# Output tiles of the last block in column parts, each part with its own PSUM tile

## The chip, the cores and the metric

The kernel runs on one core of a Trainium2 chip. The metric is the device time of one execution in microseconds (us), median of several. The profile's span is some 1.8 us shorter than the timed execution (924.2 us against 926.03 for the same one).

Engines: TensorE (PE), VectorE (DVE), ScalarE (ACT), GpSimd (POOL), SyncE (SP, which issues most transfers). A q behind a name (SPq, ACTq) is that engine's instruction queue. "L539" is line 539 of the kernel.

## The reference

A layer norm, an attention over the last 512 keys of a cache with 32 heads of 192, and a feed-forward branch that gates it:

```python
xn = _layernorm(x, axis=-1)                       # x: 1 x 2048 x 640
s = _A_ref(xn, A_k_cache, A_v_cache, A_wq, A_wo)  # attention, last step: o @ wo
g = _silu(_B_ref(xn, B_w_gate, B_w_up, B_w_down))
return x + s * g
```

Only the last step matters here: the output projection `o @ wo`, the product with `g`, and the sum with `x`.

## The kernel before

The 2048 rows are 16 row tiles of 128, in 4 blocks of 4. I call them by block and tile: "3,1" is tile 1 of block 3, the last block. The heads are handled in 16 pairs. Each pair's share of the projection is added to `sacc`; for the last pair it comes straight from PSUM. For blocks 2 and 3 the last two pairs are accumulated together in PSUM (`late`), so such a tile takes 12 matmuls of 320 columns. By then `sacc` holds `sum * g + x` of the earlier pairs, so a tile is finished by one product and one sum:

```python
def wo_last(b, qt, eng):
    i, t = last * NB + b, 4 * b + qt
    ...
    split = b == NB - 1 and qt == 3
    sc = None if split else mm_tile() if b >= 2 and qt % 2 == 0 else sc_tile()
    ps = [(mm_tile()[:, 0, :] if split else sc[:, n, :])[:, 0:HD] for n in range(2)]
    for n, cols in enumerate(halves):
        if late(i):
            wo_mm(ps[n], i - NB, qt, n, end=False)
        wo_mm(ps[n], i, qt, n, first=not late(i))
        if split:
            nc.vector.tensor_tensor(s_f[:, n, :], ps[n], g2[:, t, cols], ALU.mult)
            nc.vector.tensor_tensor(ob[:, cols], s_f[:, n, :], sacc[:, t, cols], ALU.add)
            (nc.scalar if n else nc.sync).dma_start(out=..., in_=ob[:, cols])
    if split:
        return
    nc.vector.tensor_tensor(s_f[:], sc[:, :, 0:HD], g2[:, t, :]..., ALU.mult)   # product
    eng.tensor_tensor(ob[:], s_f[:]..., sacc[:, t, :], ALU.add)                 # sum
    stores.append((t, ob))
...
for b in (2, 3):
    for qt in range(4):
        store(0 if (b, qt) == (3, 3) else 3)
        wo_last(b, qt, V if b == 3 and qt % 2 == 0 else G)      # V VectorE, G GpSimd
```

`sc_tile()` and `mm_tile()` hand out two kinds of PSUM tile, two of each, which together fill PSUM. Only the last tile, 3,3, works in two halves, both in `mm` tiles.

The softmax here doesn't subtract the row's maximum and nothing guards it: scores larger than these inputs give would overflow.

## Time and profile before

| What | Number |
|---|---|
| Time, median | 925.96 us (3 runs, 925.85 to 926.03) |
| Span of the profile | 924.2 us |
| TensorE busy | 916.6 us, 99% |
| GpSimd busy | 100.1 us, 11%, most of it at the end |
| First matmul of tile 3,0 | at 912.44 us |
| Last store issued | at 921.39 us |

The part that the change touches is what I call the **tail**: from the first matmul of tile 3,0 to the end of the span, 924.2 - 912.44 = 11.76 us. It is read from two places of one profile, and the span has one decimal, so it is good to about 0.05 us. The prediction below shows the lines of this stretch.

### The profile page before, as it was taken

The page shows a single profiled execution, that of the slowest core. Times are in us where ns is not written, and L with a number is a line of the kernel's source. Part 1 is how long each engine was busy: PE and PEld are TensorE (multiplying, and loading weights), DVE is VectorE, ACT ScalarE, POOL GpSimd, SP SyncE. Part 2 cuts the span into 40 slices and gives each one's busy share as a digit, 9 for nine tenths or more (in the row PEclk, how much of TensorE's full clock was granted, in tenths as well). Part 3 has the DMA queues.
Part 4 walks back from the last instruction along what each step waited for, and adds up shares of the span by engine and source line. Part 5 has one row for each costly group of instructions (what it writes and reads, how often), then busy time and mean ns, then how long its engine had stood idle before and what let it go on. Part 6 is the DMA issues. An engine that isn't in the chain of part 4 may idle for free.

```text
span 924.2 us, 25783 instructions
## 1 busy us (share of the span) xinstructions
PE 916.6 (99%) x11101; PEld 622.6 (67%) x11101; DVE 576.1 (62%) x844; ACT 473.8 (51%) x847; POOL 100.1 (11%) x387
## 2 busy tenths in 40 slices
PE   9999999999999999999999999999999999999997
PEld 5455555575858585868686767676767777776665
DVE  6433331467676767676666667676767676767655
ACT  4222223546464656555556465655555555656561
POOL 0000000000000000000000000000000000002977
PEclk9999999999999999999999999999999999999999
DMA  9321510044544443444636252635371717162624
GB/s 297 74 54 35 114 35 1 1 81 86 83 83 80 86 80 86 72 94 66 100 59 107 57 109 53 112 50 116 45 121 40 126 37 129 35 132 74 145 47 140
DMA packets 243810, 77.18 MB, mean 84 GB/s; under 512 B 224624, under 2 KB 243696, under 8 KB 243696
## 3 DMA queue, kind: packets, MB, share of 16 engines
q1 hardware_dynamic: 242640, 74.72, 40.7%
q8 instruction: 87, 1.43, 0.7%
q10 hardware_dynamic: 1056, 0.82, 0.3%
q14 instruction: 27, 0.22, 0.1%
HBM read 39.45 MB, written 2.62 MB: 46 GB/s over the span
## 4 chain that ended last, share of the span: by engine, by line
PE 98%; DMA 1%; DVE 1%; ACTq 0%; issue 0%; ACT 0%; DVEq 0%
PE mm L430 22%; PE sc L565 19%; PE sc L444 18%; PE mm L470 16%; PE sc L276 11%; PE mm L298 6%; PE sc L539 3%; PE mm L522 2%; PE mm L539 1%; DMA wu_sb<-in_B_w_up_dram 1%; PE mm L276 0%; PE mm L311 0%; PE sc L522 0%; PE sc L470 0%; PE mm L444 0%
## 5 line engine op out<-in xcount | busy, mean ns | idle before, releaser
L448 ACT ACTIVATE p_t<-sc 128x1024 bf16<-128x1024 f32 x254 | 253.0, 1022 | 128.9 <-PE sc L444 128.9
L435 DVE TENSOR_REDUCE qT<-mm 128x512 bf16<-128x1024 f32 x189 | 230.9, 1223 | 91.6 <-PE mm L430 89.2
L500 ACT ACTIVATE O_b<-mm,r 128x192 bf16<-128x192 f32 x486 | 164.6, 421 | 183.6 <-issue 162.4
L430 PE MATMUL mm<-xnT,wq_p 64*128 64x512 bf16 x1890 | 240.0, 376 | 0.0
L590 DVE TENSOR_TENSOR sacc<-sacc,sc 128x640 f32<-128x640 f32 x200 | 164.2, 821 | 89.5 <-PE sc L565 89.5
L565 PE MATMUL sc<-wo_p,OT_b 64*128 64x320 bf16 x2592 | 217.0, 296 | 0.0
L444 PE MATMUL sc<-qT,khat 64*128 64x512 bf16 x1524 | 198.1, 376 | 0.5 <-DVE sacc L588 0.5
L470 PE MATMUL mm<-V_p,p_t 64*128 64x193 bf16 x3520 | 186.2, 242 | 0.1
L470 PEld LDWEIGHTS <-p_t 64*128 64x128 bf16 x3584 | 162.4, 93 | 12.9 <-issue 0.6
L430 PEld LDWEIGHTS <-wq_p 64*128 64x128 bf16 x1890 | 104.7, 94 | 95.7 <-issue 0.5
L565 PEld LDWEIGHTS <-OT_b 64*128 64x128 bf16 x2592 | 139.4, 94 | 22.2
L444 PEld LDWEIGHTS <-khat 64*128 64x128 bf16 x1536 | 85.1, 94 | 80.1 <-issue 0.7
L553 POOL MEMSET turn_t<- 128x1 f32 x328 | 32.2, 98 | 697.0 <-PE mm L470 474.6
L284 DVE TENSOR_TENSOR hT<-sc,sg 128x512 bf16<-128x512 f32 x46 | 31.7, 690 | 85.2 <-ACT sg L283 85.1
L283 ACT ACTIVATE sg<-sc 128x512 bf16<-128x512 f32 x46 | 27.3, 596 | 72.4 <-PE sc L276 72.4
L276 PE MATMUL sc<-xnT,wu_sb 128*128 128x512 bf16 (+1 forms) x260 | 59.1, 354 | 0.2 <-DMA wu_sb<-in_B_w_up_dram 0.2
L276 PE MATMUL sc<-xnT,wg_sb 128*128 128x512 bf16 (+1 forms) x260 | 59.2, 354 | 0.1
L298 PE MATMUL mm<-wd_sb,hT 128*128 128x320 bf16 x384 | 56.6, 299 | 0.0
L489 DVE RECIPROCAL r<-mm 128x4 f32<-128x4 f32 x124 | 22.7, 183 | 47.8 <-PE mm L470 36.3
L298 PEld LDWEIGHTS <-hT 128*128 128x128 bf16 x384 | 37.6, 98 | 18.9
L276 PEld LDWEIGHTS <-wu_sb 128*128 128x128 bf16 x285 | 26.3, 98 | 27.2 <-DMA wu_sb<-in_B_w_up_dram 0.4
L276 PEld LDWEIGHTS <-wg_sb 128*128 128x128 bf16 x285 | 26.4, 98 | 23.1 <-issue 0.2
(68 smaller groups left out, 372.9 us busy)
## 6 DMA issues: line engine op xcount, KB each, us to landing
wo_p<-in_A_wo_dram SPq DMA_DIRECT2D x16, 480.0 KB, 4.2
K_p<-in_A_k_cache_dram SPq DMA_DIRECT2D x32, 192.0 KB, 3.3
V_p<-in_A_v_cache_dram SPq DMA_DIRECT2D x32, 192.0 KB, 3.1
wq_p<-in_A_wq_dram SPq DMA_DIRECT2D x64, 80.0 KB, 3.2
wq_p<-in_A_wq_dram SPq DMA_DIRECT2D x16, 160.0 KB, 3.4
x_r<-in_A_x_dram SPq DMA_DIRECT2D x16, 160.0 KB, 3.9
x_t<-in_A_x_dram SPq DMA_DIRECT2D x14, 160.0 KB, 3.0
OT_b<-O_b SPq DMA_TRANSPOSE x124, 2.8
```

Of the source, the lines that this page charges most:

```text
L276: nc.tensor.matmul(out, w_sb[:, c, f * P : (f + 1) * P], xnT[:, c, qc], start=(c == 0), stop=(c == NC - 1),)
L298: nc.tensor.matmul(dn[:, 0:HD], hTs[b][:, f, ti * P : (ti + 1) * P], wd_sb[:, f, cols], start=(f == 0), stop=(f == NF - 1),)
L430: nc.tensor.matmul(q_ps[:, h, :], pairs[pr]["wq"][r, c, j * P : (j + 1) * P], xnT[r, c, b * 512 : (b + 1) * 512], start=(c == 0), stop=(c ...
L435: nc.vector.reduce_sum(qTs[i][:, j, :], q_ps[:, :, :].rearrange("p h n -> p n h"), axis=AX.X)
L444: nc.tensor.matmul(sc[:, h, :], khat[r, j, ks], qT[r, j, :], start=(j == 0), stop=(j == 2))
L448: nc.scalar.activation(p_t[:, :, :], sc[:, :, :], ACT.Exp, scale=scale)
L470: m = nc.tensor.matmul(acc[:, k, h * 256 : h * 256 + Dh + 1], Ps[i][kc][r, h, qt * P : (qt + 1) * P], V_p[r, kc, h, 0 : Dh + 1], start=(p ...
L500: nc.scalar.activation(O_b[:, qt, h, :], a_k[:, h, 0:Dh], ACT.Copy, scale=r[:, k, h, :])
L539: nc.tensor.matmul(ps, OTs[i][:, 3 * qt + j, :], pairs[i // NB]["wo"][:, j, n * HD : (n + 1) * HD], start=(first and j == 0), stop=(end an ...
L553: st["turn"] = nc.gpsimd.memset(turn_t[:], 0.0)
L565: m = nc.tensor.matmul(ps[:, n, 0:HD], OTs[i][r, 3 * qt + j, :], pairs[i // NB]["wo"][r, j, n * HD : (n + 1) * HD], start=(turn == 0 and j ...
L590: nc.vector.tensor_tensor(s_t, s_t, sc[:, :, 0:HD], ALU.add)
```

## The change

Its intent: finish the last rows sooner after TensorE is done, by working on pieces. All four tiles of block 3 are made in column parts. Every part has its own PSUM tile, the first of a tile an `mm`, the second an `sc`. VectorE multiplies each part as soon as it is there, and the sums are dealt out by part to GpSimd (G) and VectorE (V). The last tile is cut into 384 and 256 columns, the 256 part's store on ScalarE's queue. The core of the diff:

```diff
+    def wo_parts(qt, parts):
+        i, t, c0 = NS - 1, 4 * (NB - 1) + qt, 0
+        ob = finp.tile([P, D], bf, name="ob", bufs=4)
+        s_f = finp.tile([P, D], f32, name="s_f", tag="s_f", bufs=4)
+        for n, (width, eng, queue) in enumerate(parts):
+            cols, c0 = slice(c0, c0 + width), c0 + width
+            ps = (sc_tile() if n else mm_tile())[:, 0, 0:width]
+            wo_cols(ps, i - NB, qt, cols, end=False)
+            wo_cols(ps, i, qt, cols, first=False)
+            nc.vector.tensor_tensor(s_f[:, cols], ps, g2[:, t, cols], ALU.mult)
+            eng.tensor_tensor(ob[:, cols], s_f[:, cols], sacc[:, t, cols], ALU.add)
+            if queue:
+                queue.dma_start(out=out2[t * P : (t + 1) * P, cols], in_=ob[:, cols])
+        if not queue:
+            stores.append((t, ob))
...
-    for b in (2, 3):
-        for qt in range(4):
-            store(0 if (b, qt) == (3, 3) else 3)
-            wo_last(b, qt, V if b == 3 and qt % 2 == 0 else G)
+    for qt in range(4):
+        store(3)
+        wo_last(2, qt)
+    for qt, engs in enumerate(((G, V), (G, G), (V, G))):
+        store(2 - qt)
+        wo_parts(qt, [(HD, eng, None) for eng in engs])
+    store(0)
+    wo_parts(3, ((384, G, nc.sync), (D - 384, V, nc.scalar)))
```

The rest of the diff only takes the split case out of `wo_last` and gives the matmul helper its columns. The stores of finished rows are also asked for earlier (`store(2 - qt)` where it was `store(3)`).

More of the change, by code (lines that the diff above doesn't have):

```diff
@@ L535, in late, with wo_cols @@
         return i // NB >= NPAIR - 2 and i % NB >= 2
-    def wo_mm(ps, i, qt, n, first=True, end=True):
+    def wo_cols(ps, i, qt, cols, first=True, end=True):
         for j in range(3):
             nc.tensor.matmul(
-                ps, OTs[i][:, 3 * qt + j, :], pairs[i // NB]["wo"][:, j, n * HD : (n + 1) * HD],
+                ps, OTs[i][:, 3 * qt + j, :], pairs[i // NB]["wo"][:, j, cols],
                 start=(first and j == 0), stop=(end and j == 2),
             )
+    HALVES = [slice(n * HD, (n + 1) * HD) for n in range(2)]
     def follows(m, earlier):
@@ L602, in wo_full @@
         for n in range(2):
-            wo_mm(sc[:, n, 0:HD], i, qt, n)
+            wo_cols(sc[:, n, 0:HD], i, qt, HALVES[n])
         s_t = sacc[:, t, :].rearrange("p (n d) -> p n d", n=2)
@@ L618, with wo_last @@
     stores = []
-    def wo_last(b, qt, eng):
+    def wo_last(b, qt):
         i, t = last * NB + b, 4 * b + qt
@@ L623, in wo_last @@
         s_f = finp.tile([P, 2, HD], f32, name="s_f", bufs=4)
-        halves = [slice(n * HD, (n + 1) * HD) for n in range(2)]
-        split = b == NB - 1 and qt == 3
-        sc = None if split else mm_tile() if b >= 2 and qt % 2 == 0 else sc_tile()
-        ps = [(mm_tile()[:, 0, :] if split else sc[:, n, :])[:, 0:HD] for n in range(2)]
-        for n, cols in enumerate(halves):
-            if late(i):
-                wo_mm(ps[n], i - NB, qt, n, end=False)
-            wo_mm(ps[n], i, qt, n, first=not late(i))
-            if split:
-                nc.vector.tensor_tensor(s_f[:, n, :], ps[n], g2[:, t, cols], ALU.mult)
-                nc.vector.tensor_tensor(ob[:, cols], s_f[:, n, :], sacc[:, t, cols], ALU.add)
-                (nc.scalar if n else nc.sync).dma_start(
-                    out=out2[t * P : (t + 1) * P, cols], in_=ob[:, cols]
-                )
-        if split:
-            return
+        sc = mm_tile() if b == 2 and qt % 2 == 0 else sc_tile()
+        for n, cols in enumerate(HALVES):
+            if late(i):
+                wo_cols(sc[:, n, 0:HD], i - NB, qt, cols, end=False)
+            wo_cols(sc[:, n, 0:HD], i, qt, cols, first=not late(i))
         nc.vector.tensor_tensor(
@@ L642, in wo_last @@
         )
-        eng.tensor_tensor(ob[:], s_f[:].rearrange("p n d -> p (n d)"), sacc[:, t, :], ALU.add)
+        G.tensor_tensor(ob[:], s_f[:].rearrange("p n d -> p (n d)"), sacc[:, t, :], ALU.add)
         stores.append((t, ob))
+    def wo_parts(qt, parts):
[13 more added lines that the diff above has]
+            stores.append((t, ob))
     def store(left):
@@ L720 @@
         for k in range(2):
-            wo_last(b, 2 * q2 + k, G)
+            wo_last(b, 2 * q2 + k)
         if more:
             pv_full(i + more[0], more[1])
-    for b in (2, 3):
-        for qt in range(4):
-            store(0 if (b, qt) == (3, 3) else 3)
-            wo_last(b, qt, V if b == 3 and qt % 2 == 0 else G)
+    for qt in range(4):
[6 more added lines that the diff above has]
+    wo_parts(3, ((384, G, nc.sync), (D - 384, V, nc.scalar)))
 _INS = ['A_x', 'A_k_cache', 'A_v_cache', 'A_wq', 'A_wo', 'B_x', 'B_w_gate', 'B_w_up', 'B_w_down']
```

## The prediction

> **What bounds the kernel now.** I read the page first (busy shares, slices), then the chain that ended last in the stretch from 905 us, then the timeline of that stretch, then the DMA issues. The page:
>
> ```profile
> span 924.2 us, 25783 instructions
> PE 916.6 (99%) x11101; PEld 622.6 (67%) x11101; DVE 576.1 (62%) x844; ACT 473.8 (51%) x847; POOL 100.1 (11%) x387
> POOL 0000000000000000000000000000000000002977
> ...
> PEclk9999999999999999999999999999999999999999
> ```
>
> TensorE is busy for 99% of the span at full clock, so all but about 8 us is TensorE work, and the change leaves that work alone: it still runs 48 projection matmuls for block 3 with the same weight loads and the same total of columns. GpSimd (POOL) is busy for 11% of the span, nearly all of it in the last four slices (23 us each): that is the stage the change touches. The end of the chain (columns: start us, length us, what):
>
> ```profile
> 912.60 1.63 PE mm L539 x12
> 914.23 1.63 PE sc L539 x12
> 915.86 1.64 PE mm L539 x12
> 917.50 0.03 issue
> ...
> 917.60 0.84 DVE s_f L640
> ...
> 918.46 0.04 DVE ob L643
> ...
> 919.43 0.49 DVE s_f L633
> 919.94 0.49 DVE ob L634
> 920.43 0.41 DVE s_f L633
> 920.87 0.49 DVE ob L634
> ```
>
> TensorE carries the chain until 917.50. From there VectorE carries it to 921.36, then the last store runs to 924.2. So only 6.7 us of 924.2 are open to this change, 0.7%. The timeline shows what VectorE and GpSimd do there (start us, us, engine, line, operation):
>
> ```profile
> 909.75 6.04 POOL L643 TENSOR_TENSOR ob<-s_f,sacc 128x640 bf16<-128x640 f32 x4
> 915.20 1.27 DVE L643 TENSOR_TENSOR ob<-s_f,sacc 128x640 bf16<-128x640 f32 x1
> 916.40 0.81 DVE L640 TENSOR_TENSOR s_f<-sc,g 128x640 f32<-128x640 f32 x1
> 917.29 1.54 POOL L643 TENSOR_TENSOR ob<-s_f,sacc 128x640 bf16<-128x640 f32 x1 [1.50 <-DVE s_f L640]
> 918.46 1.05 DVE L643 TENSOR_TENSOR ob<-s_f,sacc 128x640 bf16<-128x640 f32 x1
> 918.48 0.57 PE L539 MATMUL mm<-wo_p,OT_l 128*128 128x320 bf16 x3 [0.17 <-DVE s_f L640]
> 921.39 0.37 ACTq L635 DMA_DIRECT2D out_dram<-ob  x1
> ```
>
> Three things are to be seen. GpSimd is booked without a gap until 915.79 (909.75 + 6.04), with the sums of block 2. The two VectorE sums of 640 columns took 1.27 and 1.05 us, though two of 320 columns took 0.49 each. And TensorE lost a little before its last half tile: the first matmul there waited for VectorE to read tile 3,2.
>
> **What the skill says.** (1) The Trainium skill, "SBUF — State Buffer", section "SBUF: two separate sides": VectorE and GpSimd share a port pair under an exclusive lock; a VectorE instruction with two SBUF inputs and a GpSimd one that reads SBUF do not share, whichever starts first has it for its whole length. The trace agrees, closely: the first 640 sum ended at 916.47, 0.68 us after GpSimd's at 915.79; the second at 919.51, also 0.68 us after GpSimd's at 918.83. A VectorE sum that meets GpSimd therefore sits until GpSimd is done and then needs 0.68 us. The products `s_f`, one input from PSUM, took 0.82 us with GpSimd busy or not. (2) "GPSIMD Engine Reference", section "3.1 Elementwise — side-by-side cycle accounting": about 2.6 cycles per element for two inputs against about 1 on VectorE. The trace: 1.50 us from start to start on GpSimd against 0.82 us on VectorE for 640 columns. (3) "Perfetto Trace Analysis", section "DMA Instruction — HWDGE (DVE, Sync)": an issue's span leaves out the movement of data, and completion to HBM can be long. The trace: 0.37 us of issue, 1.6 us to landing.
>
> **The change, part by part.** Durations used: a half tile (six matmuls of 320) is 0.815 us on TensorE (1.63/2). I take 0.98 and 0.65 us for 384 and 256 columns, in proportion. A product starts 0.27 us after the next matmuls of TensorE could start (912.44 to 912.71). A 320 product lasts 0.48 us, the next independent instruction starts 0.41 us after it, a dependent sum 0.51 us after. A free VectorE sum of 320 is 0.49 us; after GpSimd lets go it needs half of 0.68, 0.34 us, and 0.27 us for 256 columns. For GpSimd no 320 sum is in the trace: from 1.50 us with a small fixed part I estimate 0.80 us for 320 and 0.95 for 384.
>
> Removed: the two 640 sums on VectorE in tiles 3,0 and 3,2 (1.27 + 1.05 us), and one 640 sum on GpSimd. Added: two 320 sums and one 256 sum on VectorE, four 320 sums and one 384 sum on GpSimd. VectorE's sums fall from 1920 columns to 896, GpSimd's rise from 640 to 1664, about 2.5 us more work for an engine that is not free before 915.79. Six instructions more in the pair of engines, and no more DMA.
>
> What moves on TensorE: with six parts ring-buffered over two kinds of PSUM tile, each part waits for a reader two tiles back. The wait of 0.17 us (0.33 with the refill, 918.48 against 918.15) goes away. TensorE's last group should end at 917.33 + 1.63 = 918.96 instead of 919.30. That alone would be 0.3 us.
>
> What happens after it, if the lock changes hands at each instruction (case A). Product 3,0 first part 913.53, second 914.34; its VectorE sum starts 914.85, is held to 915.79, ends 916.13. GpSimd's 3,0 sum then runs to 916.95. Products 3,1 at 916.15 and 916.58, 3,2 first at 917.0. VectorE's 3,2 sum starts 917.5, is held by GpSimd's 3,1 first part to 917.75, ends 918.09. GpSimd's second 3,1 part ends 918.89, 3,2 second 919.69. Product of 384 at 918.58, of 256 at 919.23 (TensorE end 918.96 + 0.27), ready 919.64. The last VectorE sum gets the lock at 919.69 and ends 919.96; GpSimd's 384 sum then ends 920.92. Or the other way about: GpSimd first, then 0.27 us for VectorE, 920.93. Either way the last issue starts near 920.97 instead of 921.39. From issue to end I keep 2.81 us (924.2 - 921.39). Sum: 923.78, or **-0.4 us**.
>
> **Rivals.** Case B, a wait takes the place of the one removed: GpSimd's next instruction starts before the lock is free, since its starts are 1.50 us apart and its spans 1.55 us. A waiting VectorE then loses to every queued GpSimd sum. VectorE's 3,0 sum would be held to 916.57 (915.77 + 0.80) and end 916.91; products 3,1 at 916.83 and 917.24, 3,2 first at 917.65; its sum is held by both GpSimd parts of 3,1 to 918.93 and ends 919.27; last products 919.6 and 920.1; GpSimd's 3,2 part to 920.52, 384 part to 921.43, VectorE's last sum 921.70, issue 921.74. That is **+0.35 us**. For it: the overlapping spans. Against it: in the trace, VectorE's held sums ended 0.68 us after the holder in both cases; but no second GpSimd instruction was queued then, so this does not decide.
>
> Case C, little contention: GpSimd runs back to back from 915.79 (917.37, 918.17, 918.97 at the ends of its parts but for the first), the 384 sum waits for its product at 919.13 and ends 920.08; VectorE's last sum ends 920.35, issue 920.39, **-1.0 us**. For it: this is what the split into narrower parts aims at. Against it: both VectorE sums of the old kernel that could meet GpSimd did.
>
> Case D: the landing of the smaller store hides or undoes it. The last store falls from 80 to 64 KB and the other grows to 96 KB; issue to landing was 1.6 us at 80 KB and 1.8 at 160 KB, so 16 KB is worth about 0.03 us. I leave it out.
>
> **Range and chances.** I give A 0.45, B 0.35, C 0.20: -0.18 + 0.12 - 0.20 = -0.26, so 925.96 - 0.26 = 925.7 us. The range runs from C (924.9) to B with the spread of the old runs, 0.1 us (926.4). A change of 2% is 18.5 us, more than the whole tail. Faster by over 2%: 0.005; within 2%: 0.99; slower by over 2%: 0.005.
>
> **What would show it.** Everything up to about 912.4 us must look as before. Right: no TensorE wait at the last half tile; VectorE's sums lengthened when GpSimd is busy, ending 0.34 us after it; the last issue near 921.0. If VectorE's 3,0 sum ends near 916.9, it is B; if all three VectorE sums are near 0.5 us, C. The prediction is wrong if a GpSimd sum of 320 costs much more than 0.8 us, if products with a PSUM input are held as well, or if the stretch from last issue to end is not 2.8 us.

## The result, and the profile after

The changed kernel took 925.26 us (median of 5 runs, 925.09 to 925.64), the kernel before 925.85 (5 runs, 925.52 to 926.03). The ratio is 0.9994, 95% interval 0.998 to 1.0007. A ratio is the mean time of one kernel's fast runs over that of the other's of the same rounds, so not quite the ratio of the medians quoted. By the 2% measure this is the same time; what is left is a difference of about 0.6 us, with both kernels scattered by 0.5 us.

The page after, its head and GpSimd's row of busy tenths:

```profile
span 923.8 us, 25792 instructions
...
POOL 0000000000000000000000000000000000002978
```

0.4 us less span, and one tenth more of GpSimd in the last slice. Before taking the 0.4 us for the change, look where it arises. TensorE's third set of transposes, ten microseconds into the kernel, and its first matmuls of tile 3,0, first in the profile before (start us, length us, engine, line, operation):

```profile
10.63 0.45 PE L264 MATMUL tp<-ident,xn 128*128 128x128 bf16 x5
...
912.44 0.57 PE L539 MATMUL mm<-wo_p,OT_l 128*128 128x320 bf16 x3
```

and in the profile after:

```profile
10.36 0.45 PE L264 MATMUL tp<-ident,xn 128*128 128x128 bf16 x5
...
912.16 0.57 PE L539 MATMUL mm<-wo_p,OT_l 128*128 128x320 bf16 x3
```

A lead of 0.27 us is there after 10 us, in code that the change does not touch, and 0.28 us at tile 3,0. TensorE, 99% busy in between, carries it to the end. Over all the profiles tile 3,0 starts anywhere from 911.99 to 912.97 us. That scatter is larger than the effect sought, so from here on the tail is compared: 923.8 - 912.16 = **11.64 us** after, 11.76 us before. In these two profiles the tail is 0.12 us shorter.

The end of the chain of work that ended last, after (start us, length us, what):

```profile
915.58 0.83 PE mm L539 x6
916.41 0.03 issue
...
917.94 0.42 DVE ob L649
918.36 0.48 DVE s_f L648
...
919.11 0.85 POOL ob L649
919.97 1.13 POOLq L766
```

Before, TensorE handed over to VectorE at 917.50, 5.06 us after the start of tile 3,0, and VectorE carried the chain to its last sum. Now TensorE leaves the chain at 916.41, 4.25 us after that start, and the end goes through GpSimd. The timeline of the two engines after:

```profile
913.97 1.57 POOL L634 TENSOR_TENSOR ob<-s_f,sacc 128x640 bf16<-128x640 f32 x1
914.51 2.20 DVE L649 TENSOR_TENSOR ob<-s_f,sacc 128x320 bf16<-128x320 f32 x1
915.47 0.90 POOL L649 TENSOR_TENSOR ob<-s_f,sacc 128x320 bf16<-128x320 f32 x1
...
917.19 3.91 POOL L649 TENSOR_TENSOR ob<-s_f,sacc 128x320 bf16<-128x320 f32 x4 [0.83 <-DVE s_f L648]
...
919.66 0.58 DVE L649 TENSOR_TENSOR ob<-s_f,sacc 128x256 bf16<-128x256 f32 x1
920.28 0.37 ACTq L651 DMA_DIRECT2D out_dram<-ob  x1
921.12 0.33 SPq L651 DMA_DIRECT2D out_dram<-ob  x1
```

VectorE's first sum, 320 columns, takes 2.20 us; one of the same size took 0.49 us before, where nothing was in its way. It ends at 916.71, 0.34 us after GpSimd's second instruction of this list, at 916.37. So it was held through two GpSimd instructions. Meanwhile VectorE makes no product for GpSimd, which then stands idle for 0.83 us. The last issue, on SyncE's queue, comes 8.96 us after the start of tile 3,0; before it was 921.39 - 912.44 = 8.95. So up to the last issue nothing is won here; that it is this hold which costs the gain, the profiles with a shorter hold below show. The 0.12 us lie after the last issue, in a stretch of 2.68 us (2.81 before) that scatters by about 0.1 us over the profiles below.

### The profile page after: what moved, and what is told of

Its sections match the earlier page's. It is cut to its first block, busy times and chain, and to the rows that moved or that the text cites. A ratio compares the mean times of both kernels' runs of the same rounds, so it can differ in the third digit from the quotient of the medians.

```text
span 923.8 us, 25792 instructions
## 1 busy us (share of the span) xinstructions
PE 916.7 (99%) x11101; PEld 626.0 (68%) x11101; DVE 576.2 (62%) x846; ACT 473.8 (51%) x847; POOL 103.3 (11%) x391
## 4 chain that ended last, share of the span: by engine, by line
PE 98%; DMA 1%; DVE 0%; POOLq 0%; issue 0%; POOL 0%; DVEq 0%
PE mm L430 22%; PE sc L567 19%; PE sc L444 18%; PE mm L470 16%; PE sc L276 11%; PE mm L298 6%; PE sc L539 3%; PE mm L522 2%; PE mm L539 1%; DMA wg_sb<-in_B_w_gate_dram 1%; PE mm L276 0%; PE mm L311 0%; DMA x_t<-in_A_x_dram 0%; PE sc L522 0%; PE sc L470 0%; DVE s_f L648 0%
```

## The experiments

They ran in three batches of four, each batch on one chip with the kernel before timed beside it. "Tail" is as defined above; "last issue" is the issue of the last store, counted from the start of tile 3,0.

| Run | What | Tail, us | Last issue, us | Median time, us | Ratio |
|---|---|---|---|---|---|
| (before) | first profile | 11.76 | 8.95 | 925.96 | |
| e6_b_again | before, again | 11.73 | 8.98 | 925.93 | 1.0001 |
| (after) | first profile | 11.64 | 8.96 | 925.26 | 0.9994 |
| e1_after_again | changed, again | 11.15 | 8.40 | 925.29 | 0.9993 |
| e12_after_third | changed | 11.11 | 8.42 | (one run) | |
| e13_after_fourth | changed | 11.10 | 8.37 | (one run) | |
| e2_psum_only | TensorE's wait removed alone | 11.77 | 8.96 | 926.19 | 1.0002 |
| e3_last_v | last sums both on VectorE | 11.07 | 8.38 | 925.77 | 0.9997 |
| e7_halves | last tile 320 + 320 | 11.08 | 8.34 | 925.53 | 0.9996 |
| e5_first_gg | first sum to GpSimd | 11.55 | 8.90 | 925.92 | 0.9999 |
| e8_product_in_psum | changed, VectorE sums from PSUM | 10.69 | 7.97 | 924.89 | 0.9988 |
| e10_gv | that, 3,2 exchanged | 10.75 | 7.79 | 925.37 | 0.9992 |
| e9_b_product_in_psum | before, VectorE sums from PSUM | 11.84 | 9.05 | 925.92 | 1.0001 |
| e11_b_psum_own | that, without TensorE's wait | 11.57 | 8.86 | 925.85 | 0.9997 |

The 95% intervals are about 0.0013 to either side, so one ratio alone rarely decides, and I go by the tails. Each tail is read from one profile; two profiles of the same code in which the engines took the same turns differ by 0.01 to 0.05 us. By "lock theory" the expectations mean what the prediction says under (1): a VectorE sum with two inputs in SBUF and a GpSimd sum wait for each other.

### Both kernels again: e1_after_again, e6_b_again

No edit in either.

> The changed kernel once more, unaltered. I measure the tail: from the first projection matmul of tile 3,0 to the end of the span; it was 11.76 us before (924.2 - 912.44) and 11.64 us changed (923.8 - 912.16). Theory 1: the tail is the same from run to run, and of the 0.4 us between the two profiles only 0.12 us belongs to the change; the other 0.28 us was there at tile 3,0 already and comes from the first loads of the kernel. Then the tail here is 11.64 within 0.05 us, while the start of tile 3,0 may lie anywhere from 912.1 to 912.5, and the ratio of times is near 0.9998. Rival: the change saves about 0.5 us in a usual run, as the medians 925.85 and 925.26 say; then the ratio is 0.9994 to 0.9995 again and the tail shorter than 11.5 us.

> The kernel before once more, as a control with its own profile. Theory 1: tail 11.76 us within 0.05, start of tile 3,0 from 912.1 to 912.5 us, ratio 1.000 within 0.0003. Rival (its first profile was not typical): a tail longer than 11.9 us.

The control came out as expected in tail and ratio: 11.73 us and 1.0001. The start of tile 3,0 did not: it was 912.97 us here and 912.75 in e1_after_again, both outside the 912.1 to 912.5 that I had written. For the changed kernel theory 1, that the tail is the same from run to run, fell: it was 11.15 us, 0.49 us shorter than in the first profile of the same code, and the ratio 0.9993. The lines of VectorE's first and last sums, and of the last issue, in this run:

```profile
915.11 1.34 DVE L649 TENSOR_TENSOR ob<-s_f,sacc 128x320 bf16<-128x320 f32 x1
...
919.93 1.18 DVE L649 TENSOR_TENSOR ob<-s_f,sacc 128x256 bf16<-128x256 f32 x1
...
921.15 0.37 ACTq L651 DMA_DIRECT2D out_dram<-ob  x1
```

The same instruction, started at the same place (2.36 us after tile 3,0 against 2.35), took 1.34 us instead of 2.20. GpSimd's line shows why:

```profile
914.57 1.53 POOL L634 TENSOR_TENSOR ob<-s_f,sacc 128x640 bf16<-128x640 f32 x1
916.06 1.11 POOL L649 TENSOR_TENSOR ob<-s_f,sacc 128x320 bf16<-128x320 f32 x1
```

VectorE's sum ended at 916.45, 0.35 us after GpSimd's 640 sum at 916.10: it got its turn at the first change of instruction. Now GpSimd's next sum was the one held, 1.11 us instead of some 0.86. The last sum, 256 columns, ends 0.28 us after GpSimd's 384 sum (919.85 + 0.98 = 920.83), held as well. So the tail of the changed kernel has two lengths, depending on who gets the turn. The rival of theory 1, that the change usually saves more than its first profile shows, stands.

### How often: e12_after_third, e13_after_fourth

The changed kernel twice more, one look each.

> The changed kernel again, for one more look at how VectorE's sum of tile 3,0 and GpSimd take turns. In the first profile it was passed over at the change from GpSimd's last 640 sum to its first 320 sum and took 2.20 us (tail 11.64); in three others with the same code up to there it got its turn and took 1.34 to 1.35 us (tail 11.07 to 11.15). If the turn is left to chance, either of the two may show; if only two lengths are possible, nothing between 1.4 and 2.1 us does, and the tail goes with it.

> As the run before it: VectorE's sum of tile 3,0 takes either 1.35 us, with a tail near 11.15, or 2.20 us, with a tail near 11.64; the longer one should come with longer GpSimd spans (1.57 us for 640 columns) and the shorter with 1.53 to 1.54[...].

The first VectorE sum in e12_after_third, then in e13_after_fourth:

```profile
914.35 1.37 DVE L649 TENSOR_TENSOR ob<-s_f,sacc 128x320 bf16<-128x320 f32 x1
```

```profile
914.76 1.32 DVE L649 TENSOR_TENSOR ob<-s_f,sacc 128x320 bf16<-128x320 f32 x1
```

The sum took 1.37 and 1.32 us, the tails were 11.11 and 11.10 us. So of four looks at the changed kernel one has the long hold, three the short one; in e3_last_v and e7_halves, whose code is the same up to there, it took 1.35 us as well. GpSimd's 640-column spans were 1.57 us in the one long case and 1.52 to 1.56 in the short ones. The order is as I expected, but the 1.56 of e12_after_third misses the 1.53 to 1.54 that I had written for the short hold, and 1.56 against 1.57 with one long case is too little to show that GpSimd's length decides. What decides the turn stays open.

### TensorE's wait alone: e2_psum_only

On the kernel before:

```diff
-ps = [(mm_tile()[:, 0, :] if split else sc[:, n, :])[:, 0:HD] for n in range(2)]
+ps = [((sc_tile() if n else mm_tile())[:, 0, :] if split else sc[:, n, :])[:, 0:HD] for n in range(2)]
```

> The kernel before, with only the second half of the last tile put into the other kind of PSUM tile, so that TensorE no longer waits for the reader of tile 3,2; sums and stores are as before. Theory 1: the wait goes and TensorE ends 0.33 us sooner, but VectorE is behind by then (its last four instructions ran without a gap from 919.43 us), so the tail stays at 11.76 us within 0.05. Rival: the removed wait is what the change gains; then the tail is 11.43 us.

```profile
918.14 0.57 PE L539 MATMUL sc<-wo_p,OT_l 128*128 128x320 bf16 x3
```

The wait went: the last half tile's matmuls start at 918.14, 5.71 us after tile 3,0, instead of 6.04. VectorE's last four instructions did not move (919.42 - 912.43 = 6.99 us against 919.43 - 912.44 = 6.99), and the tail is 11.77 us. Taking this wait away gains nothing by itself, because VectorE was behind. (Only this half tile was moved; the own PSUM tiles of the other parts are not tested here.)

### The last sum and the widths: e3_last_v, e7_halves

```diff
-wo_parts(3, ((384, G, nc.sync), (D - 384, V, nc.scalar)))
+wo_parts(3, ((384, V, nc.sync), (D - 384, V, nc.scalar)))     # e3_last_v
+wo_parts(3, ((HD, G, nc.sync), (HD, V, nc.scalar)))           # e7_halves
```

> The changed kernel, with the 384-column sum of the last tile moved from GpSimd to VectorE. In the changed kernel that sum ended last, 8.92 us after the start of tile 3,0. Lock theory: VectorE's 384 sum becomes ready about 7.15 us after the start of tile 3,0 while GpSimd works on tile 3,2 until 7.8, so it is held, ends near 8.2, and the 256 product and sum follow to about 9.0: the tail stays between 11.5 and 11.8 us. Rival without a hold: the 384 sum ends near 7.7, the 256 sum near 8.4, and the tail is 11.1 to 11.2 us.

> The changed kernel, last tile in parts of 320 and 320 columns instead of 384 and 256. It is also a third sample of the same code up to the last tile: does VectorE's first sum (tile 3,0) end 1.3 us or 2.2 us after its start? Lock theory: the last VectorE sum waits for GpSimd's last one, which gets 0.16 us shorter, and then needs 0.34 instead of 0.27 us: tail 0.1 us shorter than the changed kernel's of the same kind, 11.05 us where the first hold is 1.3 us and 11.55 where it is 2.2 us. Rival, that the narrow last part is what saves time: tail 0.15 us longer, 11.3 or 11.8.

For e3_last_v my range for the lock theory (11.5 to 11.8) missed, since I had worked it out from the first profile, the one with the long hold; the number (11.07) fell near the rival's. But the rival said "no hold", and there was one: the 384 sum lasted 0.83 us, from 919.45 to 920.28, and ended 0.42 us after GpSimd's sum of tile 3,2 (919.00 + 0.86). Against the changed kernel with the short hold (11.10 to 11.15) the tail is equal within what can be read. Moving the sum gains nothing.

In e7_halves the last VectorE sum (1.05 us, from 919.87) ends 0.35 us after GpSimd's last (919.72 + 0.85). Tail 11.08 us, as the lock theory had it (11.05). The choice of 384 and 256 over two halves is worth nothing measurable here.

### A hold moved: e5_first_gg

```diff
-for qt, engs in enumerate(((G, V), (G, G), (V, G))):
+for qt, engs in enumerate(((G, G), (G, G), (V, G))):
```

> The changed kernel, with the VectorE sum of tile 3,0 moved to GpSimd, so that VectorE meets no hold there. VectorE's products then follow TensorE. GpSimd has 320 sums queued from 3.3 to about 6.6 us after the start of tile 3,0, and VectorE's sum of tile 3,2 becomes ready at about 4.9 us in the middle of them. If GpSimd's queued sums always win, that sum is held until 6.6 us or later and the tail is over 12 us; if VectorE gets its turn at the next change of instruction, the sum lasts 0.5 to 1.2 us and the tail is 11.1 to 11.5 us.

VectorE's products followed TensorE as expected, and the hold moved to the sum of tile 3,2:

```profile
916.72 0.86 POOL L649 TENSOR_TENSOR ob<-s_f,sacc 128x320 bf16<-128x320 f32 x1
917.50 1.25 DVE L649 TENSOR_TENSOR ob<-s_f,sacc 128x320 bf16<-128x320 f32 x1
917.54 0.86 POOL L649 TENSOR_TENSOR ob<-s_f,sacc 128x320 bf16<-128x320 f32 x1
```

The two GpSimd instructions ran from 916.72 to 917.58 and from 917.54 to 918.40; the sum ended at 918.75, 0.35 us after the second. It neither waited for the whole queue (tail over 12 us) nor got off with 1.2 us: 1.25 us and a tail of 11.55, just past the edge of the second range. Both that range and the first kind of theory are missed, the first by far. It started 0.04 us before the second GpSimd instruction and did not get in ahead of it: a second case of VectorE passed over at a change of instruction.

### The lock taken away: e8_product_in_psum

If the hold comes from two SBUF inputs, a sum with one input from PSUM must not feel it, just as VectorE's products do not (0.82 us with GpSimd busy or not). So, for VectorE's sums, the product goes back into its PSUM tile:

```diff
-nc.vector.tensor_tensor(s_f[:, cols], ps, g2[:, t, cols], ALU.mult)
-eng.tensor_tensor(ob[:, cols], s_f[:, cols], sacc[:, t, cols], ALU.add)
+prod = ps if eng is V else s_f[:, cols]
+nc.vector.tensor_tensor(prod, ps, g2[:, t, cols], ALU.mult)
+eng.tensor_tensor(ob[:, cols], prod, sacc[:, t, cols], ALU.add)
```

> The changed kernel; where VectorE makes the sum, the product is written back into its own PSUM tile instead of SBUF, so that the sum has only one SBUF input (sacc). Lock theory: such a sum does not need what GpSimd holds. All three VectorE sums last 0.40 to 0.50 us whatever GpSimd does, GpSimd's 320 sums follow one another at 0.82 us without one of 1.1 us, the last store issues near 7.7 us after the start of tile 3,0 (8.96 and 8.40 in the two profiles of the changed kernel), and the tail is 10.4 to 10.6 us (11.64 and 11.15 there, 11.76 before). Rival (VectorE is simply slowed by a busy GpSimd, or in-order waits of another kind make it late): sums of VectorE stay lengthened and the tail is 11.1 us or more.

```profile
914.83 0.49 DVE L650 TENSOR_TENSOR ob<-sc,sacc 128x320 bf16<-128x320 f32 x1
...
917.52 0.49 DVE L650 TENSOR_TENSOR ob<-mm,sacc 128x320 bf16<-128x320 f32 x1 [0.27 <-POOL ob L650]
...
919.60 0.42 DVE L650 TENSOR_TENSOR ob<-sc,sacc 128x256 bf16<-128x256 f32 x1
```

```profile
914.25 1.54 POOL L634 TENSOR_TENSOR ob<-s_f,sacc 128x640 bf16<-128x640 f32 x1
915.75 1.69 POOL L650 TENSOR_TENSOR ob<-s_f,sacc 128x320 bf16<-128x320 f32 x2
```

The first sum runs wholly inside GpSimd's 640 sum (914.25 to 915.79) and takes 0.49 us. None of GpSimd's 320 sums takes 1.1 us any more. The tail is 10.69 us, a little over my 10.4 to 10.6: the last issue came at 7.97 us, not 7.7, since GpSimd made the 384 sum right after the second part of tile 3,2. The five timed runs (924.58 to 925.13) all lie below all nine of the kernel before (925.69 to 926.37), ratio 0.9988, 95% interval 0.9975 to 1.0; the medians differ by 1.10 us, the tails by 1.07. By the 2% measure it is the same time. Its tail is shorter than in any profile of the two kernels; its times overlap with those of the changed kernel, which was timed on another chip (924.93 to 925.95). It also shows the cause: the same work on the same engines in the same order, only the place of the product differs.

### One exchange more: e10_gv

```diff
-for qt, engs in enumerate(((G, V), (G, G), (V, G))):
+for qt, engs in enumerate(((G, V), (G, G), (G, V))):
```

> The kernel with VectorE's products in PSUM, and in tile 3,2 the two sums exchanged: GpSimd makes the first part's, VectorE the second's. There GpSimd sat idle for 0.30 us before the second part's product and then had it and the 384 sum in a row, so the 384 sum, the last store issued, was ready 7.95 us after the start of tile 3,0. Now its queue runs through to about 6.7 us and the 384 sum ends near 7.7. The last VectorE sum stays where TensorE's end puts it (7.6). Lock theory: tail 10.4 to 10.5 us against 10.69. Rival (the end is set by TensorE and the landing alone): 10.69 again.

GpSimd's queue did run through and the last issue came sooner, 7.79 us instead of 7.97, though not at 7.7. The tail did not follow: 10.75 us, the same as 10.69 within the reading. A miss for the expectation. Its rival fits: ScalarE's store, behind TensorE's last part, is issued at 7.72 us here and 7.65 us in e8_product_in_psum, so SyncE's store no longer stands alone at the end. The profiles show where the 0.18 us went: the two last stores took 1.8 and 1.9 us from issue to landing, 1.6 both in e8_product_in_psum. That they slowed each other is not shown.

### The same edit without column parts: e9_b_product_in_psum, e11_b_psum_own

On the kernel before, VectorE's sums (tiles 3,0, 3,2 and 3,3) read their product from PSUM; e11_b_psum_own adds the edit of e2_psum_only. The cut below leaves out the same edit for tile 3,3; `halved` only views 640 columns as 2 x 320.

```diff
-nc.vector.tensor_tensor(s_f[:], sc[:, :, 0:HD], g2[:, t, :]..., ALU.mult)
-eng.tensor_tensor(ob[:], s_f[:]..., sacc[:, t, :], ALU.add)
+prod = sc[:, :, 0:HD] if eng is V else s_f[:]
+nc.vector.tensor_tensor(prod, sc[:, :, 0:HD], halved(g2[:, t, :]), ALU.mult)
+eng.tensor_tensor(halved(ob[:]), prod, halved(sacc[:, t, :]), ALU.add)
```

> The kernel before (no column parts for tiles 3,0 to 3,2), with the same one edit: VectorE's sums in tiles 3,0, 3,2 and 3,3 read their product from PSUM. Lock theory: the 640 sums take about 0.82 us instead of 1.27 and 1.05; the product of tile 3,2 ends at 5.98 us after the start of tile 3,0 as before, since it waits for TensorE, so the wait of TensorE stays; the last four instructions start 0.23 us sooner: last issue near 8.7 (8.95 before), tail 11.5 us. If the lock is all that mattered, the tail would be as short as with column parts and the same edit (10.5 us); if the columns are what matters, 11.5.

> The kernel before, with VectorE's products in PSUM and the second half of the last tile in the other kind of PSUM tile, so that TensorE's wait of 1.10 us, which the edit alone brought in, goes as well. Neither TensorE waits nor the lock are left then; only the columns differ from the changed kernel with the same edit. If the columns carry part of the gain: VectorE has 640 sums of tiles 3,0 and 3,2 and both sums of the last tile to make, its last issue comes near 8.8 us after the start of tile 3,0, tail 11.5 us. If lock and wait were all: 10.7 us.

The 640 sums took 0.82 and 0.83 us instead of 1.27 and 1.05, as the lock theory says. But e9_b_product_in_psum did not get shorter: 11.84 us where I had written 11.5. A wait took the place of the hold. The first 640 sum, and the wait:

```profile
915.07 0.82 DVE L643 TENSOR_TENSOR ob<-mm,sacc 128x640 bf16<-128x640 f32 x1
...
919.22 0.58 PE L539 MATMUL mm<-wo_p,OT_l 128*128 128x320 bf16 x3 [1.10 <-DVE ob L643]
```

The last half tile uses the PSUM tile of 3,2, and that is now free only after the sum, not after the product. I had overlooked that a product in PSUM keeps its tile longer. With the other kind of tile (e11_b_psum_own) the wait is gone and the tail is 11.57 us, near the 11.5 expected. So without the lock and without the wait, whole tiles gain 0.19 us; with column parts on top 10.69 us are reached, 0.88 us less. Two things differ there, not only the columns as my expectation says: the pieces are narrower, and VectorE makes 896 columns of sums instead of 1920 while GpSimd makes the rest at the same time. No run deals out whole tiles in another way, so what each of the two is worth stays open.

## Why the prediction was right or wrong

The range, 924.9 to 926.4 us, includes the measured 925.26; the time, 925.7, was 0.4 us too long, and the chances, 0.99 for within 2%, were right. None of this was a hard test: the range also includes the kernel before (925.96), the whole tail is 1.3% of the time, and 925.7 is the mean of three cases, so it describes none of them. That the first profile's span, 923.8 us, is just case A's 923.78 is luck: 0.28 us of its lead were there at tile 3,0, and its first hold was case B's. The case I called most likely, case A with -0.4 us, is the one that most looks show, with -0.6. Point by point:

- **What bounds the kernel, and that only the tail is open**: right. Outside the tail the two profiles differ by a scatter of the start that both kernels have (e1, e6, e12, e13).
- **TensorE's wait goes, worth 0.3 us "alone"**: half right. It went (e2_psum_only, and the changed kernel's last tile starts 4.89 us after tile 3,0 in e1_after_again, as worked out; in the first profile, with the long hold, it starts at 5.01). But "alone" it is worth nothing: tail 11.77 us. TensorE is not what the end waits for at that point.
- **The lock, 0.34 us after GpSimd lets go**: right. The first sum ended 0.34 to 0.35 us after the instruction that held it, in the first profile and in e1_after_again. Take the second SBUF input away and the hold is gone (e8_product_in_psum).
- **GpSimd at 0.80 us per 320 sum and 0.95 per 384**: 0.82 us from start to start, and 0.98 us long.
- **Case A, -0.4 us**: the mechanism was right in three of four looks; the size was off. The last issue came at 8.37 to 8.42 us after tile 3,0, where the prediction's 920.97 is 8.53. The term mis-sized is the change of turns, which I had put end to end while neighbours overlap (VectorE's product after its first sum starts at 3.63 us instead of 3.71, GpSimd's 384 sum at 7.10 instead of 7.25). The rest, 0.06 to 0.12 us, lies in the stretch from the last issue to the end: 2.69 to 2.75 us where I kept the 2.81 of one profile. The smaller store is not shown to be the reason: with a last store of 80 KB the stretch was 2.71 to 2.81 us (2.71 in e11_b_psum_own, 2.74 in e7_halves), with 96 KB, in the first profile, 2.68.
- **Case B, +0.35 us**: its first step, VectorE held to 4.47 us after tile 3,0, is what the first profile shows (4.55 us). Its second step, that a waiting VectorE *then* loses to every queued GpSimd sum, failed: in the same profile the sum of tile 3,2 took 0.49 us, and the queued GpSimd sum was the one held (1.14 us); the last VectorE sum took 0.58. So the last issue came at 8.96 us, not at 9.30, and the tail was 0.12 us shorter than before rather than 0.35 longer.
- **The list of work**: "Removed" leaves out the two 320 sums of tile 3,3, which the totals of columns (1920 to 896) do count; and by the prediction's own figures GpSimd gets 2.65 us more work (4 x 0.80 + 0.95 - 1.50), not about 2.5. Neither changes a case.
- **Case C, -1.0 us**: not reached by this change; about what the version without the lock reaches (11.76 - 10.69 = 1.07 us).

What is open: why VectorE was passed over at a change of instruction, once in four looks at the changed kernel and once in e5_first_gg. In the changed kernel, start times within 0.01 us of each other gave both outcomes. I also tried no run in which each part's own PSUM tile is undone in the changed kernel, so its share there is only argued from e2_psum_only and e9_b_product_in_psum.

## What to carry to other kernels

When two engines wait for each other, as VectorE and GpSimd do here in sums with both inputs in SBUF, dealing the sums out to both buys less than the sum of their speeds; look for the instruction whose length exceeds that of its twin elsewhere in the trace and see whose end it follows. An operand left in PSUM can take an instruction out of that competition, at the price of holding the PSUM tile longer, so check who needs the tile next. For effects under a microsecond compare a stretch inside the profile, counted from a fixed instruction, and look at more than one profile of the same code.

## What the Trainium skill lacked or had wrong

- "SBUF — State Buffer", section "SBUF: two separate sides", says that whichever starts first gets the shared pair for the whole instruction. For two instructions the runs agree (a VectorE sum of 320 columns took 1.34 us behind GpSimd and 0.49 us without it; a GpSimd one 1.11 us behind VectorE and 0.86 without). The page does not say who is next when GpSimd has another instruction queued: with equal start times a waiting VectorE got the turn at once in three of four looks at the changed kernel (1.32 to 1.37 us) and was passed over in one (2.20 us), although its record begins 0.96 us before that of the GpSimd sum that went first (914.51 against 915.47). In e5_first_gg it was passed over too. So the start that the profile shows does not tell who goes first.
- The same page, section "Who interferes with whom", says that a VectorE instruction with at most one SBUF input does not contend, and the runs agree. It does not draw from it that a product may be left in PSUM to keep the following sum out of the lock, nor what that costs. Here the three sums took 0.49, 0.49 and 0.42 us beside a busy GpSimd and the tail fell from 11.1 to 10.69 us; where the PSUM tile was needed next, TensorE waited 1.10 us for it.
- "GPSIMD Engine Reference", section "3.1 Elementwise — side-by-side cycle accounting", gives about 2.6 cycles per element for two inputs but no fixed part of a whole GpSimd instruction in nanoseconds. From starts 1.50 us apart at 640 columns and 0.82 at 320 I estimate 2.1 ns per element and 0.14 us fixed.
